# Linear attention and MLP on one core: squares of the decay taken early, two transposed tiles copied by two engines, three store pairs merged

## The chip, the cores and the metric

The kernel runs on one core of a Trainium2 chip. The metric is the device time of that core in microseconds (us); lower is better. A *time* below is that of a whole execution; a *span* is the stretch from the first to the last instruction in a trace, and the time is about 1.8 us longer (200.52 us beside a span of 198.7 us for the kernel before).

## The reference, cut to what matters

Linear attention with one decay factor per head, in blocks of 64 tokens, followed by a two-layer MLP.

```python
# q, k, v: (4 batches, 8 heads, 768 tokens, 64); lam: (8,), 0.97 to 0.99
for b in range(12):                      # blocks of 64 tokens
    intra = (qb @ kb.T * Dmask) @ vb      # Dmask = lam**(i - j), 0 above the diagonal
    inter = (qb * lam_pow) @ kv_state
    out[block] = intra + inter
    kv_state = lam**64 * kv_state + (kb * rev_pow).T @ vb
# x: (3072, 512), the heads of a token side by side
h = x @ w_in                              # (3072, 2048)
g = 0.5*h*(1 + tanh(c*(h + 0.044715*h**3)))
return g @ w_out                          # (3072, 512) float32
```

## The kernel before

The attention runs in 24 steps of 128 tokens. The start of the kernel computes powers of lam: `dq` for q, its inverse `dv` for v, and lam to the 128th (seven squarings) as the decay of the state, which is laid out as a masked tile `lumask` and a plain tile `lamu`. Each step multiplies q by `dq` (VectorE), copies k (ScalarE), multiplies v by `dv` (GpSimd). For steps 0 to 8, TensorE then transposes q and k into the PSUM tile `Tps`, and a copy moves them to `qkT` in SBUF. The MLP's matmuls fill TensorE from about 16 us on.

```python
    def square(i):
        pin(nc.vector.tensor_tensor(sq[i + 1][:], sq[i][:], sq[i][:], ALU.mult))

    def odd(hs):
        pin(nc.vector.tensor_tensor(dq[:, hs, 1], dq[:, hs, 0], lam_bc[:, hs], ALU.mult))

    def chunk_decay():                                   # the state's decay, 4 elements a partition
        l3 = sq[7][:].rearrange("p (hp two) -> p hp two", two=2)
        for hl in range(2):
            r = slice(64 * hl, 64 * hl + 64)
            pin(nc.vector.tensor_copy(out=lumask[r, :, hl], in_=l3[r, :, hl]))
        pin(nc.vector.tensor_tensor(lamu[:], lumask[:, :, 0], lumask[:, :, 1], ALU.add))

    for i in range(5):
        square(i)
    odd(halves[0])
    # ... cut ...
    def stage_t(s):                                      # transposes of step s and their copy
        # ... cut: eight transposes into Tps, which is one PSUM tile: q into Tps[:, 0], k into Tps[:, 1]
        o = qkp.tile([P, 2, 2, 2, P], FP16, tag="qkT", name=f"qkT_{s}")
        if s in (2, 3):
            pin(nc.scalar.activation(out=o[:, 0], in_=Tps[:, 0], func=AF.Copy))
            pin(nc.vector.tensor_copy(out=o[:, 1], in_=Tps[:, 1]))
        elif s in (1, 5, 6, 8):
            pin(nc.scalar.activation(out=o[:], in_=Tps[:], func=AF.Copy))
        else:
            pin(nc.vector.tensor_copy(out=o[:], in_=Tps[:]))
    # ... cut ...
            def store(T, ps=slice(0, NP), es=slice(0, 2)):   # output tile T of token group g
                r = row0 + T * HN
                rows = out[r : r + HN, :].rearrange("(p q) (e d) -> q p e d", q=P, e=2)
                for i in range(ps.start, ps.stop):           # one transfer of 256 KB each (128 KB for half of es)
                    pin(nc.sync.dma_start(out=rows[:, i, es], in_=out_tile(T)[:, i, es, :]))
    # ... cut: the order of the work from here ...
    idle(4)              # matmuls on ones, whose result nobody reads: they keep TensorE busy
    prep(0)              # q, k, v of step 0
    stage_t(0)
    idle(1)
    square(5)
    square(6)
    prep(1)
    chunk_decay()
    idle(2)
    R(0, None)           # scores, products and mask of step 0
    stage_t(1)
    idle(5)
    # ... cut ...
```

`pin` keeps the order of the program on each engine.

## Time and profile before

| | kernel before |
|---|---|
| time, median of six (beside the kernel after) | 201.07 us (200.94 to 201.34) |
| profiled execution: time, span | 200.52 us, 198.7 us |
| TensorE busy | 191.4 us of 198.7 (96%) |
| stores of the output | 23 transfers of 256 KB and two of 128 KB; the last store is one of the two |

The list of DMA issues (output and input, queue, count, size, median us from issue to landing) has the stores that the change merges:

```profile
out_dram<-o SPq DMA_DIRECT2D x23, 256.0 KB, 4.2
```

First, the idle matmuls of the first 13 us (the view of one source line: count, then durations in ns as shortest / median / longest, then the first and the last start in us). One of 512 columns takes about 635 ns before TensorE's clock rises and 380 after (back to back, one starts every 0.43 us before the rise and every 0.22 us after it), so the median tells that most of them ran after the rise:

```profile
L182 PE MATMUL idle<-ones x19: 379/380/635, 1.5 to 11.7; 128*128 128x512 f16 x19
```

Second, three pieces of the chain that ended last (start us, us, engine, tile, line): the first long run of MLP matmuls (24.50 here; the timeline, which the prediction reads, has its first matmul at 24.34), then the transposes of step 4, where the prediction expected a delay to be absorbed, and what follows them:

```profile
24.50 6.91 PE Hps L524 x32
...
39.17 0.61 PE Tps L293 x8
...
39.78 1.73 PE O2ps L539 x8
```

### The profile page before, as it was taken

The page shows a single profiled execution, that of the slowest core. Times are in us where ns is not written, and L with a number is a line of the kernel's source. Part 1 is how long each engine was busy: PE and PEld are TensorE (multiplying, and loading weights), DVE is VectorE, ACT ScalarE, POOL GpSimd, SP SyncE. Part 2 cuts the span into 40 slices and gives each one's busy share as a digit, 9 for nine tenths or more (in the row PEclk, how much of TensorE's full clock was granted, in tenths as well). Part 3 has the DMA queues.
Part 4 walks back from the last instruction along what each step waited for, and adds up shares of the span by engine and source line. Part 5 has one row for each costly group of instructions (what it writes and reads, how often), then busy time and mean ns, then how long its engine had stood idle before and what let it go on. Part 6 is the DMA issues. An engine that isn't in the chain of part 4 may idle for free.

```text
span 198.7 us, 5952 instructions
## 1 busy us (share of the span) xinstructions
PE 191.4 (96%) x2444; PEld 139.2 (70%) x2444; DVE 153.3 (77%) x299; ACT 122.1 (61%) x246; POOL 73.6 (37%) x85
## 2 busy tenths in 40 slices
PE   7889999999999999999999999999999999999992
PEld 1446544456888898654588754578888888888881
DVE  5898723689999889949898478999768996588530
ACT  2463878466883674587735577844768845779211
POOL 6593223457457733435633465055002030002000
PEclk9999999999999999999999999999999999999999
DMA  6999999999999999999774999340220300020214
GB/s 172 290 326 386 385 386 384 295 286 310 333 254 253 235 297 216 237 290 215 190 174 93 278 294 200 86 51 0 53 85 24 108 6 0 0 109 16 93 46 167
DMA packets 61755, 37.87 MB, mean 191 GB/s; under 512 B 17568, under 2 KB 54688, under 8 KB 61728
## 3 DMA queue, kind: packets, MB, share of 16 engines
q1 hardware_dynamic: 61184, 37.23, 72.4%
q8 instruction: 19, 0.31, 0.7%
q10 hardware_dynamic: 544, 0.26, 0.5%
q14 instruction: 8, 0.07, 0.1%
HBM read 27.26 MB, written 6.29 MB: 169 GB/s over the span
## 4 chain that ended last, share of the span: by engine, by line
PE 93%; DVE 2%; ACT 1%; POOL 1%; issue 1%
PE Hps L524 24%; PE MX L601 17%; PE MY L601 9%; PE HX L692 7%; PE O2ps L539 7%; PE MW L601 4%; PE Hps L783 4%; PE S L322 4%; PE HY L692 4%; PE OK L380 2%; PE Tps L293 2%; PE OK L371 2%; PE HW L692 2%; PE idle L182 1%; POOL dq L216 1%; PE OK L357 1%
## 5 line engine op out<-in xcount | busy, mean ns | idle before, releaser
L524 PE MATMUL Hps<-xT,w_in 128*128 128x512 f16 (+1 forms) x288 | 51.0, 332 | 0.0
L483 POOL TENSOR_TENSOR u<-t,lumask 128x256 f16<-128x256 f32 x40 | 29.9, 761 | 49.1 <-DVE t L476 33.7
L524 PEld LDWEIGHTS <-w_in 128*128 128x128 f16 x288 | 27.8, 98 | 18.8
L528 ACT ACTIVATE gT<-Hps 128x512 f16<-128x512 f32 x56 | 33.0, 596 | 10.9 <-PE Hps L524 10.4
L332 DVE TENSOR_TENSOR PT<-S,mask 128x512 f16<-128x512 f32 x48 | 30.5, 682 | 8.0 <-PE S L322 7.9
L601 PEld LDWEIGHTS <-gs 128*128 128x128 f16 x320 | 31.2, 98 | 3.6
L257 POOL TENSOR_TENSOR v<-v,dv 128x512 f16<-128x512 f32 x24 | 29.6, 1239 | 6.9 <-DMA v<-in_v_dram 6.5
L601 PEld LDWEIGHTS <-gT 128*128 128x128 f16 x240 | 23.2, 98 | 3.6 <-ACT gT L528 0.5
L601 PE MATMUL MX<-w_sum,gs 128*128 128x256 f16 x160 | 21.4, 273 | 0.0
L275 ACT ACTIVATE qk<-k 128x512 f16<-128x512 f32 x24 | 15.0, 626 | 7.6 <-DMA k<-in_k_dram 7.6
L270 DVE TENSOR_TENSOR qk<-q,dq 128x512 f16<-128x512 f32 x23 | 19.1, 832 | 0.5 <-DMA q<-in_q_dram 0.5
L645 POOL TENSOR_TENSOR o<-u,q 128x512 f32<-128x512 f32 (+1 forms) x5 | 5.3, 1054 | 37.8 <-ACT u L618 37.8
L571 DVE TENSOR_TENSOR gs<-gT 128x1024 f16<-128x1024 f16 (+1 forms) x24 | 17.8, 749 | 1.7 <-ACT gT L528 1.7
L457 ACT ACTIVATE xT<-OK 128x256 f16<-128x256 f32 x34 | 13.0, 456 | 6.4 <-PE OK L380 6.2
L539 PE MATMUL O2ps<-w_out,gT 128*128 128x512 f16 x64 | 14.6, 379 | 0.0
L692 PEld LDWEIGHTS <-ws 128*128 128x128 f16 x128 | 12.5, 97 | 1.8
L618 ACT ACTIVATE u<-MX 128x256 f32<-128x256 f32 x18 | 6.9, 383 | 10.1 <-PE MX L601 10.1
L476 DVE SCALAR_TENSOR_TENSOR t<-t,lamu,OK 128x64 f32<-128x64 f32 x48 | 11.0, 275 | 1.1 <-PE OK L357 0.2
L322 PEld LDWEIGHTS <-qkT 64*64 64x64 f16 x384 | 6.1, 106 | 7.5 <-issue 2.3
L539 PEld LDWEIGHTS <-gT 128*128 128x128 f16 x64 | 6.1, 98 | 6.6
L601 PE MATMUL MY<-w_out,gs 128*128 128x256 f16 x80 | 10.7, 273 | 0.0
L601 PE MATMUL MX<-w_sum,gT 128*128 128x256 f16 x80 | 10.4, 273 | 0.0
(94 smaller groups left out, 311.8 us busy)
## 6 DMA issues: line engine op xcount, KB each, us to landing
q<-in_q_dram SPq DMA_DIRECT2D x24, 256.0 KB, 5.2
k<-in_k_dram SPq DMA_DIRECT2D x24, 256.0 KB, 5.1
v<-in_v_dram SPq DMA_DIRECT2D x23, 256.0 KB, 5.3
out_dram<-o SPq DMA_DIRECT2D x23, 256.0 KB, 4.2
wo<-in_moe_w_out_dram SPq DMA_DIRECT2D x4, 1024.0 KB, 9.5
wi<-in_moe_w_in_dram SPq DMA_DIRECT2D x4, 512.0 KB, 8.0
wi<-in_moe_w_in_dram SPq DMA_DIRECT2D x2, 1024.0 KB, 12.7
v<-in_v_dram ACTq DMA_DIRECT2D x1, 256.0 KB, 4.2
```

The source lines that it names most:

```text
L257: pin(nc.gpsimd.tensor_tensor(wide(tv[:]), ld32[s][2][:], decay(dv, s), ALU.mult))
L270: pin(q_eng.tensor_tensor(wide(tq), q32[:], decay(dq, s), ALU.mult))
L275: pin(nc.scalar.activation(out=wide(tk), in_=k32[:], func=AF.Copy))
L322: pin(nc.tensor.matmul(Sps[hl][half64(c), hp, jk, :], o[half64(hl), 1, jk, hp, half64(c)], o[half64(hl), 0, :, hp, half64(c)], start=True, ...
L332: pin(nc.vector.tensor_tensor(t[:, hl].rearrange("p b c d -> p b (c d)"), Sps[:].rearrange("p b c d -> p b (c d)"), mask[:].unsqueeze(1).t ...
L483: pin(nc.gpsimd.tensor_tensor(u[:], state[half][:].unsqueeze(2).to_broadcast([P, 2, 2, D]), lumask[:, 2 * half : 2 * half + 2, :].unsqueez ...
L524: pin(nc.tensor.matmul(by_block(Hps[:, i, :]), w_in16[:, c, f * P : (f + 1) * P], x(c), start=(c == 0), stop=(c == NC - 1)))
L528: pin(nc.scalar.activation(out=dst, in_=Hps[:], func=AF.Gelu_apprx_tanh))
L539: pin(nc.tensor.matmul(O2[tau][0][:], gT[:, f % HF, f // HF, tau * P : (tau + 1) * P], w_out16[:, f, :], start=(n == 0), stop=(n == NF - 1)))
L571: pin(nc.vector.tensor_tensor(g_rows(m, i), g_rows(a, i), g_rows(b, i), op))
L601: pin(nc.tensor.matmul(dst, lhsT, rhs, start=(opens and i == 0), stop=(closes and i == HF - 1), skip_group_check=True))
L692: pin(nc.tensor.matmul(dst[:, i, :], w_in_block(a, slice(c, c + 1), slice(f * P, f * P + P))[:, 0], x_block(b, slice(c, c + 1))[:, 0], sta ...
```

## The change

Three intents. The last two squarings move ahead of step 0, and ScalarE instead of VectorE spreads the result into `lumask` and `lamu`, so that VectorE is freed between q of step 0 and q of step 1. The copies of `Tps` in steps 0 and 1 are split into a ScalarE and a VectorE half, as steps 2 and 3 already were. And three pairs of output transfers become one transfer of 512 KB each.

```diff
     def chunk_decay():
         l3 = sq[7][:].rearrange("p (hp two) -> p hp two", two=2)
-        for hl in range(2):
-            r = slice(64 * hl, 64 * hl + 64)
-            pin(nc.vector.tensor_copy(out=lumask[r, :, hl], in_=l3[r, :, hl]))
-        pin(nc.vector.tensor_tensor(lamu[:], lumask[:, :, 0], lumask[:, :, 1], ALU.add))
-
-    for i in range(5):
+        for dst in (lumask, lamu):
+            for hl in range(2):
+                r = slice(64 * hl, 64 * hl + 64)
+                to = lamu[r, :] if dst is lamu else lumask[r, :, hl]
+                pin(nc.scalar.activation(out=to, in_=l3[r, :, hl], func=AF.Copy))
+
+    for i in range(7):
         square(i)
     odd(halves[0])
@@
-        if s in (2, 3):
+        if s < 4:
             pin(nc.scalar.activation(out=o[:, 0], in_=Tps[:, 0], func=AF.Copy))
             pin(nc.vector.tensor_copy(out=o[:, 1], in_=Tps[:, 1]))
-        elif s in (1, 5, 6, 8):
+        elif s in (5, 6, 8):
@@
-                for i in range(ps.start, ps.stop):
+                whole = g == 3 or (g, T) == (4, 0)
+                for i in [ps] if whole else [slice(i, i + 1) for i in range(ps.start, ps.stop)]:
                     pin(nc.sync.dma_start(out=rows[:, i, es], in_=out_tile(T)[:, i, es, :]))
@@
     stage_t(0)
+    chunk_decay()
     idle(1)
-    square(5)
-    square(6)
     prep(1)
-    chunk_decay()
     idle(2)
```

## The prediction

> **What bounds the kernel now.** I read the page first, then the chain that ended last, then the start and the stretch around 39 us of the timeline. The page says who is busy and when:
>
> ```profile
> PE 191.4 (96%) x2444; PEld 139.2 (70%) x2444; DVE 153.3 (77%) x299; ACT 122.1 (61%) x246; POOL 73.6 (37%) x85
> ...
> PE   7889999999999999999999999999999999999992
> ...
> DMA  6999999999999999999774999340220300020214
> ...
> PE 93%; DVE 2%; ACT 1%; POOL 1%; issue 1%
> ```
>
> TensorE (PE) is full from the fourth slice on: a slice is 198.7 / 40 = 4.97 us, so only about the first 15 us have holes, and the last slice is the final store. The chain (last line) agrees. The DMA engines are at nine tenths or more from slice 2 to slice 19, which will matter. The change can therefore only pay in the first 20 us, where a step runs VectorE (q times decay) and ScalarE (k copied), eight TensorE transposes into Tps, the copy of Tps to qkT, then the scores S. The timeline of that stretch (start and duration in us, engine, line; in brackets the idle time before it and its releaser):
>
> ```profile
> 4.47 0.16 DVE L224 TENSOR_TENSOR dq<-dq,lam_bc 128x4 f32<-128x4 f32 x1
> 4.67 0.69 DVE L270 TENSOR_TENSOR qk<-q,dq 128x512 f16<-128x512 f32 x1
> ...
> 5.42 0.69 PE L293 MATMUL Tps<-ident,qk 128*128 128x128 f16 x8 [0.48 <-POOL dq L216]
> ...
> 6.14 0.69 DVE L302 COPY qkT<-Tps 128x1024 f16<-128x1024 f16 x1 [0.29 <-PE Tps L293]
> ...
> 6.75 0.36 DVE L221 TENSOR_TENSOR sq<-sq 128x8 f32<-128x8 f32 x2
> 6.88 0.26 PEld L322 LDWEIGHTS <-qkT 64*64 64x64 f16 x16 [0.63 <-DVE qkT L302]
> ...
> 7.44 0.63 ACT L275 ACTIVATE qk<-k 128x512 f16<-128x512 f32 x1 [1.79 <-DMA k<-in_k_dram]
> ...
> 8.55 1.02 ACT L300 ACTIVATE qkT<-Tps 128x1024 f16<-128x1024 f16 x1 [0.49 <-PE Tps L293]
> ...
> 9.63 0.26 PEld L322 LDWEIGHTS <-qkT 64*64 64x64 f16 x16 [0.53 <-ACT qkT L300]
> ...
> 11.51 0.60 ACT L297 ACTIVATE qkT<-Tps 128x512 f16<-128x512 f16 x1
> ...
> 12.14 0.42 DVE L298 COPY qkT<-Tps 128x512 f16<-128x512 f16 x1
> ```
>
> The two evictions to be split are at 6.14 (step 0, VectorE alone, 0.69 us) and 8.55 (step 1, ScalarE alone, 1.02 us); the scores of both wait for them. The last two lines are step 2, already split in the way the change uses: the ScalarE half ends at 12.11 and the VectorE half starts at 12.14. The halves run one after the other. VectorE's work before that copy (masking PT, from 10.72 for 1.27 us) had ended at 11.99, so the 0.15 us between is a wait for ScalarE. The built program of the changed kernel says the same: VectorE's half waits for ScalarE's semaphore in all four split steps.
>
> Then the place where the start meets the rest of the kernel:
>
> ```profile
> 38.70 0.63 ACT L275 ACTIVATE qk<-k 128x512 f16<-128x512 f32 x1 [0.75 <-DMA k<-in_k_dram]
> 38.80 0.42 PEld L293 LDWEIGHTS <-qk 128*128 128x128 f16 x4
> 39.01 0.77 PE L293 MATMUL Tps<-ident,qk 128*128 128x128 f16 x8
> 39.38 0.23 PEld L293 LDWEIGHTS <-qk 128*128 128x128 f16 x4 [0.16 <-ACT qk L275]
> ```
>
> At 38.70 ScalarE has just been given k of step 4 by a DMA; four of that step's transposes are ready, the other four wait 0.16 us for ScalarE's copy. So TensorE already arrives there 0.16 us early, and the DMA queue, saturated since about 5 us, says when it may go on.
>
> [...]this trace has 0.21 us for the one-element warm-up activation, and I use that, rounded to 0.2, for the four tiny spreads. [...] The holes here are 0.3 to 0.5 us and the page's granted clock is 9 tenths or more throughout, [...].
>
> **The change part by part.**
>
> Squares early. Before, five squares run from 3.35 to 4.33, then the odd decay waits for GpSimd's power (3.40 + 1.01 = 4.41) and starts at 4.47. Squares are 0.20 us apart (3.35, 3.56), so seven end at 4.73 and the odd decay starts at 4.76: 0.29 later. q of step 0 then ends at 5.65 instead of 5.36. Its transposes took 0.69, partly waiting for k (ScalarE, done 5.65); that wait goes and they take 0.62, as in step 2: they end at 6.32, not 6.11. Cost 0.21.
>
> First eviction. 0.69 becomes 0.60 + 0.03 + 0.42 = 1.05, cost 0.36. The scores of step 0 start at about 7.45, not 6.88: 0.57 later.
>
> VectorE afterwards. The two late squares (0.36) are gone, so q of step 1 starts at 7.40, not 7.03. ScalarE does the four spreads from 6.97 to 7.8 and reaches k of step 1 at 7.8, while its DMA landed at 7.44: a new delay of 0.36. The transposes of step 1 end at about 8.8 against 8.51, 0.3 later. Against this VectorE has lost three small instructions (two of 0.16 us and one of 0.16 us, from 7.63 to 8.15), so the masking of step 0 and the state copy keep their old times, 8.05 and 9.25.
>
> Second eviction. ScalarE's half 8.82 to 9.42, VectorE's half, behind the state copy, 9.45 to 9.87: the scores of step 1 at about 9.92 instead of 9.63. So 1.02 us on one engine becomes 1.05 on two, and the sum so far is a loss of 0.3.
>
> Down the rest of the start. Steps 2 and 3 are copied as before and inherit 0.3, except where a DMA rules: k of step 3 (12.82), v of step 3 (16.53) and the second half of the first weights (17.82) are all waited for now. In the last, eight matmuls took 1.05 us although eight of 256 columns take 0.87 elsewhere (the 49.34 piece of the chain), so about 0.1 is swallowed there. From 20 us TensorE has no hole and carries 0.2 us to 39 us. There the 0.16 us wait for k swallows nearly all. The next step's transposes (0.55 in the chain against 0.45 for later ones) may take up another few hundredths. Left at the end: 0 to 0.1 us.
>
> Stores. Three pairs of 256 KB transfers become one of 512 KB each, same bytes and same 2 KB rows. Saved: three issues of 0.37 us (median) on SyncE's queue, which nothing in the late kernel waits for; the next transposes by DMA are issued at 116.93 for scores wanted after 126. The final group keeps its stores. I count 0.
>
> Sum: 201.01 + about 0.05, so 201.05 us.
>
> **The rivals.** (a) The whole loss of 0.3 to 0.57 reaches the end, because the k wait at 39 us is released earlier than I think or ScalarE itself runs late there. For: a full TensorE passes any delay on. Against: k lands at 38.70 whatever the start does, as the casts that free the weight buffers are themselves waiting for DMA (25.93 for the last). It would give 201.3 to 201.6. (b) The change works as intended: halves overlap or the lighter VectorE shortens the chain, the start gains 0.2 to 0.3. For: VectorE loses 0.5 us of small work before the mask of step 0 and ScalarE idles 1.79 us before k. Against: the serial halves; and even then k at 38.70 holds the gain back. It would give 200.8 to 201.0. (c) Fewer, larger stores disturb or relieve the loads near 105 to 120 us. DMA is at 2 to 4 tenths there, so at most 0.1 either way. (d) The longer hole drops the clock [...], unlikely at such short holes.
>
> **Range and chances.** The three runs of before span 0.19 us. My central 201.05 with (b) as the lower edge plus noise and (a) as the upper gives 200.7 to 201.6. Two per cent is 4 us, more than the whole start has in holes, so within 2% has 0.98, and each side 0.01.
>
> **What would show it.** Right: the step-0 scores begin near 7.4, VectorE's half starts 0.03 us after ScalarE's half in steps 0 and 1, ScalarE takes k of step 1 near 7.8 with no DMA wait, the long run of matmuls from 24.3 is 0.1 to 0.3 late, and at 39.4 the k transposes wait less than 0.16 us or not at all, with everything after where it was. Wrong: the two halves overlap; the small ScalarE copies take 0.1 or 0.4; TensorE is late after 45 us by as much as at 24 us; or a new wait stands near 105 to 125 us.

## More of the kernel before

The framework closes the kernel when its tile context is left: SyncE then waits on the semaphores of the DMA transfers (in the trace of this kernel five waits on two semaphores each, begun from 195.85 to 197.45 us). That code is not the kernel's own, and the argument will come to it.

The end: the last ScalarE copy of an output tile in the timeline,

```profile
195.05 0.38 ACT L618 ACTIVATE o<-MX 128x256 f32<-128x256 f32 x1 [0.49 <-PE MX L601]
```

and SyncE's closing instructions, on the line that leaves the tile context, in the view of one source line:

```profile
L1041 SPq EVENT_SEMAPHORE  x7: 17/28/1345, 195.8 to 198.7; - x7
L1041 SPq DRAIN  x3: 7/7/122, 197.8 to 198.3; - x3
```

One of SyncE's seven semaphore waits took 1345 ns, and the first drain begins at 197.8, 122 ns long. The last copy ends at 195.43 and the span at 198.75, which is 3.31 us for the last store and the closing.

## The result, and the profile after

| | before | after |
|---|---|---|
| median of six executions, us | 201.07 | 200.43 |
| lowest to highest, us | 200.94 to 201.34 | 200.02 to 200.69 |
| ratio, 95% interval | | 0.9964 [0.9949, 0.9979] |
| profiled execution: time, span | 200.52, 198.7 | 200.68, 198.9 |

A ratio here and below is the mean time of one kernel's fast runs over that of the other's in the same rounds, so it is not quite the ratio of the medians. The kernel after is 0.64 us faster by the medians: within 2%, but just under the predicted range of 200.7 to 201.6, and on the other side of the time before.

The two profiled executions say the opposite, 0.16 us slower. That is no contradiction: before's is faster than each of its six timed executions (200.94 at the least), after's the second slowest of its six. Two traces must be read for where they differ, and the parts then weighed with the timed executions. The trace differs in three places.

The page first; it answers the prediction's first block:

```profile
PE 192.6 (97%) x2444; PEld 140.4 (71%) x2444; DVE 150.4 (76%) x297; ACT 122.8 (62%) x251; POOL 73.4 (37%) x85
...
PE   7889999999999999999999999999999999999993
...
PE 93%; DVE 3%; ACT 1%; issue 1%
```

TensorE has 1.2 us more of busy time for the same 2444 matmuls. As no matmul was added, some ran slower. Nothing else on the page gives a reason; its row of the granted clock shows nine tenths or more throughout, in both kernels.

**The start.** The timeline of the kernel after (columns as in the prediction):

```profile
4.65 0.16 DVE L224 TENSOR_TENSOR dq<-dq,lam_bc 128x4 f32<-128x4 f32 x1
...
5.58 1.04 PE L294 MATMUL Tps<-ident,qk 128*128 128x128 f16 x8 [0.65 <-DVE qk L271]
...
6.66 0.60 ACT L298 ACTIVATE qkT<-Tps 128x512 f16<-128x512 f16 x1 [0.90 <-PE Tps L294]
...
7.15 0.41 ACT L235 ACTIVATE lumask<-sq 64x4 f32<-64x4 f32 x2
...
7.29 0.42 DVE L299 COPY qkT<-Tps 128x512 f16<-128x512 f16 x1 [1.38 <-ACT qkT L298]
...
7.83 0.64 PE L323 MATMUL S<-qkT 64*64 64x128 f16 x16
...
8.03 0.63 ACT L276 ACTIVATE qk<-k 128x512 f16<-128x512 f32 x1
...
10.78 0.42 PE L323 MATMUL S<-qkT 64*64 64x128 f16 x16
```

VectorE's half of step 0 starts at 7.29, 0.03 us after ScalarE's half ends (7.26), and the same holds in step 1: the halves are serial. Two spreads take 0.41 us, and k of step 1 starts at 8.03 with no DMA wait. All this the prediction had. But the eight transposes at 5.58 took 1.04 us where before's took 0.69, and the sixteen score matmuls 0.64 where before's took 0.42. No wait stands between them; TensorE was at half clock: the idle matmuls among them, from 6.41 to 7.27, start every 0.43 us, and those from 9.68 every 0.22. The idle matmuls (the same view as before) say so too, by their median of 606 ns against 380:

```profile
L182 PE MATMUL idle<-ones x19: 379/606/634, 1.5 to 12.7; 128*128 128x512 f16 x19
```

The raw clock records of the trace give the moment of the rise: 4.87 us in the profiled execution of before, 9.48 us in that of after. The start lost 1.00 us in all (chain, the run of 32 matmuls at 25.50 and not 24.50), of which the late rise is one part and the work moved by the change another.

**At 39 us.** The chain, and from the timeline ScalarE's copy of k of step 4:

```profile
25.50 6.91 PE Hps L525 x32
...
40.18 0.45 PE Tps L294 x8
...
40.62 1.73 PE O2ps L540 x8
```

```profile
38.90 0.63 ACT L276 ACTIVATE qk<-k 128x512 f16<-128x512 f32 x1 [0.75 <-DMA k<-in_k_dram]
```

The transposes of step 4 now take 0.45 us and not 0.61: k is ready well before TensorE comes, its 0.16 us wait is gone, and the loss shrinks from 1.00 to 0.84. That is the absorption that the prediction described, by the amount it gave. The rest, 0.84 us, stays.

**The end.** It stays until the last copy of an output tile, which is 0.87 us late:

```profile
195.92 0.38 ACT L619 ACTIVATE o<-MX 128x256 f32<-128x256 f32 x1 [0.49 <-PE MX L602]
```

And yet the span is only 0.15 us longer, 198.90 against 198.75. From the end of that copy to the end of the span, before took 3.31 us and after takes 2.60: **0.71 us came back behind the last instruction that computes anything.** SyncE's closing instructions:

```profile
L1041 SPq EVENT_SEMAPHORE  x7: 17/28/28, 196.7 to 198.8; - x7
L1041 SPq DRAIN  x3: 7/7/13, 198.1 to 198.4; - x3
```

There is no long wait and no long drain. The last store itself was no faster: from the end of its issue to its completion as SyncE sees it, 1.40 us before and 1.43 after. The list of DMA issues shows the merged stores,

```profile
out_dram<-o SPq DMA_DIRECT2D x17, 256.0 KB, 3.5
out_dram<-o SPq DMA_DIRECT2D x3, 512.0 KB, 4.8
```

but these leave the core long before: the last of them is issued at 147.98 us. What they changed is how many transfers there are: 123 before, 120 after. The records of the DMA-issuing instructions carry the semaphore that each transfer raises, and these come from a ring of eight, in the fixed order 100, 102, 103, 105, 106, 107, 108, 109. With 123 transfers the last store gets the third of the ring, 103; with 120 it gets the eighth, 109. SyncE's closing code waits for them in pairs, in the same order in both traces. From the raw records, in us:

```
closing wait on       before: wait over at   after: wait over at
105 and 103           197.19  (last store)   196.7 to 196.9
106 and 102           197.2 to 197.5,        196.7 to 196.9
107 and 100             four more waits,     196.7 to 196.9
108 and 101             0.07 apart           197.5
109 and 110                                  198.08  (last store)
pause                 0.37                   0.04
first drain ends      197.97                 198.13
last store seen -> drain ends   0.78         0.05
drain ends -> span ends         0.78         0.77
```

So before, the store that finishes last is the first to be waited for, and the four waits, the pause and the drain of the closing all come after it. After, four of the five pairs of waits are done while the last store is still under way, and pause and drain add 0.05 us. The theory for the experiments, called the ring theory below: *the gain is the place of the last store in the ring; the start loses a little, and the late clock is chance.* Its rivals: the transfer theory, that larger and fewer transfers themselves relieve something; the start theory, that the start pays in most executions and the profiled one of after is unlucky; and the hole theory, that the longer hole before the first transposes (0.65 us against 0.49) delays the rise of the clock, so that the change causes it.

### The profile page after: what moved, and what is told of

It is laid out like the page before. It is cut to its first block, busy times and chain, and to the rows that moved or that the text cites.

```text
span 198.9 us, 5947 instructions
## 1 busy us (share of the span) xinstructions
PE 192.6 (97%) x2444; PEld 140.4 (71%) x2444; DVE 150.4 (76%) x297; ACT 122.8 (62%) x251; POOL 73.4 (37%) x85
## 4 chain that ended last, share of the span: by engine, by line
PE 93%; DVE 3%; ACT 1%; issue 1%
PE Hps L525 24%; PE MX L602 17%; PE MY L602 9%; PE HX L694 7%; PE O2ps L540 7%; PE MW L602 4%; PE S L323 4%; PE Hps L785 4%; PE HY L694 4%; PE Tps L294 2%; PE OK L381 2%; PE OK L372 2%; PE HW L694 2%; PE idle L182 1%; PE OK L358 1%; PE O L432 1%
## 5 line engine op out<-in xcount | busy, mean ns | idle before, releaser
L258 POOL TENSOR_TENSOR v<-v,dv 128x512 f16<-128x512 f32 x24 | 30.1, 1258 | 5.6 <-DMA v<-in_v_dram 3.7
L271 DVE TENSOR_TENSOR qk<-q,dq 128x512 f16<-128x512 f32 x23 | 18.6, 813 | 0.6 <-DMA q<-in_q_dram 0.6
```

Of the source, the lines that this page charges most:

```text
L258: pin(nc.gpsimd.tensor_tensor(wide(tv[:]), ld32[s][2][:], decay(dv, s), ALU.mult))
L271: pin(q_eng.tensor_tensor(wide(tq), q32[:], decay(dq, s), ALU.mult))
```

## The experiments

Each kernel was timed in rounds beside the kernel before on the same chip; kernels of one group share those runs of before. All outputs are right. By the rule of a 2% threshold every run below counts as the same as the kernel before; the intervals say what can be told apart. The expectations are quoted as they were before each run and may call a theory by another name. The first group is a1_stores to a4_tiny1 (before: 200.71), the second a5_split5 to b4_fill (before: 200.72), the third the rest (before: 201.08).

### The stores alone

```diff
 # the kernel before, with only the third hunk of the change
+                whole = g == 3 or (g, T) == (4, 0)
+                for i in [ps] if whole else [slice(i, i + 1) for i in range(ps.start, ps.stop)]:
-                for i in range(ps.start, ps.stop):
```

> The kernel before with the three merged store pairs alone; the start is untouched. Theory (the end of the kernel): 120 DMA transfers in place of 123 shift the ring of eight DMA semaphores by three, the last store gets the semaphore that SyncE's closing waits check last (109) in place of one that they check first (103), and the time from the last ScalarE copy to the end falls from 3.31 to about 2.6 us: 200.3 to 200.5 us, ratio 0.996 to 0.998. Rival (the start): all of the gain is made in the first 20 us and this run is at 201.0, ratio 1.000.

Measured: 200.17 us (200.08 to 201.26) beside 200.71, ratio 0.998 [0.9959, 1.0001]. One execution of six, 201.26, is a microsecond above the other five, which lie at 200.08 to 200.48, and widens the interval past 1; the times alone leave it unclear. The trace does not: the start is before's (long run at 24.52), and the closing is after's. The last copy ends at 195.73, the span at 198.32, 2.58 us, with the drain at 197.6 and no long wait:

```profile
L1042 SPq EVENT_SEMAPHORE  x7: 17/28/28, 196.1 to 198.3; - x7
```

### The start alone

The kernel after with the old store loop, the same hunk reversed.

> The changed kernel with the stores as before; only the two parts in the start. Theory: 123 transfers again, so the closing time is 3.3 us as before, and the start costs 0.2 us where TensorE's clock rises at about 5 us and 0.85 us where it rises only at about 9.5 us: 201.2 to 201.9, ratio 1.001 to 1.005. Rival: the start gains, 200.4, ratio 0.997.

Measured: 201.01 us (200.51 to 201.41), ratio 1.0013 [0.9994, 1.0031]. The closing is long again, 3.31 us, with its long wait:

```profile
L1040 SPq EVENT_SEMAPHORE  x7: 17/28/1360, 196.7 to 199.6; - x7
```

The start of the profiled execution is after's, at 25.53, with the clock rising at 9.53 us. So the start brings nothing at the end of the kernel and probably costs some tenths. The start theory falls.

### Same stores, other counts

If only the count matters, transfers that carry nothing should do as well. Five loads of 32 bytes, into a tile that nobody reads, make 128 transfers, so the last store is again the eighth of the ring; one load makes 124, the fourth. The transfer theory expects no gain of either, since no store is merged.

```diff
+    spare = const.tile([H, 8], FP32)
@@ late in the kernel, long before the last stores
+    for i in range(5):        # a3_tiny5;   range(1) in a4_tiny1
+        pin(nc.sync.dma_start(out=spare[:, i : i + 1], in_=lam.unsqueeze(1)))
     fill(20)
```

> The kernel before, start and stores untouched, with five loads of 32 bytes that nobody reads added near 140 us: 128 transfers, which by eight is the same place in the semaphore ring as 120. Theory (ring): the last store has semaphore 109 and the closing time falls to about 2.6 us although there are more transfers, not fewer: 200.3 to 200.5, ratio 0.996 to 0.998. Rival (fewer, larger stores help by themselves): no gain, 201.0, ratio 1.000 or a little over.

> As the run with five tiny loads, but one: 124 transfers, the last store has semaphore 105, which the first of the closing waits checks, as with 103 before. Theory (ring): closing time 3.3 us, 201.0, ratio 0.999 to 1.001. Rival (any shift of the instruction stream helps): 200.4.

Measured, beside 200.71: a3_tiny5 201.09 us (200.01 to 201.86), ratio 1.0018 [0.9995, 1.0041]; a4_tiny1 201.58 us (200.63 to 201.91), ratio 1.0029 [1.0005, 1.0052]. In the traces the closing follows the ring exactly: 2.61 us with five loads, 3.26 us with one. SyncE's closing with one load, where the last store raises 105 and so is in the first pair:

```profile
L1044 SPq EVENT_SEMAPHORE  x7: 17/28/28, 197.3 to 198.7; - x7
L1044 SPq DRAIN  x3: 7/7/35, 198.0 to 198.3; - x3
```

Its seven waits begin only at 197.3, and the drain follows 0.7 us later, as in before; with five loads they begin at 196.3. The profiled executions agree with that, 200.01 against 200.63 us. But four of the five other executions of each lie 0.86 us or more above the profiled one, and by the medians neither is faster than before: the times that the theory expected (200.3 to 200.5 with five loads, 201.0 with one) were missed. (The recorded ratio of a3_tiny5 seems to leave out its fastest run; the means of the listed times give 1.0008.) Between the two kernels the medians differ by 0.49 us in the expected direction, but their intervals overlap. What the small loads cost in those other executions I could not see, since only one execution of each kernel has a trace; it stays open. For that reason a cleaner way to 128 transfers followed.

```diff
 # a5_split5: five stores cut in two instead of three pairs merged
-                    pin(nc.sync.dma_start(out=rows[:, i, es], in_=out_tile(T)[:, i, es, :]))
+                    for e in (slice(0, 1), slice(1, 2)) if g == 3 or (g, T, i) == (4, 0, 0) else (es,):
+                        pin(nc.sync.dma_start(out=rows[:, i, e], in_=out_tile(T)[:, i, e, :]))
```

> The kernel before with five of its late stores cut in two each (rows of 1 KB in place of 2 KB), nothing else: 128 transfers, by eight the same place in the ring as 120. Theory (ring): from the end of the last ScalarE copy to the end of the span 2.6 us in place of 3.31, and the time as with the merged stores, 0.5 to 0.7 us under the kernel before of the same rounds (ratio 0.9965 to 0.9985). Rival (larger stores help, more and smaller ones harm): ratio 1.000 or above, closing time 3.3 us. The two runs with tiny loads showed the shorter and the longer closing time in the profile, but their timed executions were mostly 1 us longer than the profiled one, so this run repeats the test without tiny loads.

Measured: 200.24 us (200.15 to 201.82) beside 200.72, ratio 0.9985 [0.9957, 1.0013]. More and smaller stores, the opposite of the change, and the median moves by the same half microsecond as with merged ones, though the interval includes 1. The closing took 2.89 us: the last store itself took 1.73 us from the end of its issue, 0.3 longer than elsewhere, and behind it there was again no long wait. So a shorter closing needs neither fewer nor larger transfers, and for the closing the ring theory stands. That larger transfers relieve nothing elsewhere is not shown by these times. The profiled execution of this kernel, which has before's start untouched, had the clock rise at 9.38 us: that speaks against the hole theory, at least as the only cause.

The closings of all fourteen traces, from raw records (last copy's end to the span's end):

```
kernel      transfers   last store raises   closing us
before      123         103 (third)         3.31
a2_start    123         103                 3.31
b1_split    123         103                 3.31
b2_decay    123         103                 3.30
a4_tiny1    124         105 (fourth)        3.26
after       120         109 (eighth)        2.60
r_after     120         109                 2.60
a1_stores   120         109                 2.58
b4_fill     120         109                 2.58
b3_banks    120         109                 2.58
c2_idle5    120         109                 2.59
c1_best     120         109                 2.58
a3_tiny5    128         109                 2.61
a5_split5   128         109                 2.89
```

Only the third, fourth and eighth place of the ring were tried.

### The halves alone

```diff
 # the kernel before, with only the second hunk of the change
-        if s in (2, 3):
+        if s < 4:
@@
-        elif s in (1, 5, 6, 8):
+        elif s in (5, 6, 8):
```

> The kernel before with the halves of steps 0 and 1 alone; squares, spreads and stores as before. Theory (serial halves): VectorE's half of step 0 starts about 0.03 us after ScalarE's half ends and the scores of step 0 begin 0.36 us later than before; the hole of TensorE before step 0's transposes stays 0.49 us, so the clock still rises by 7.9 us at the latest; TensorE is 0.1 to 0.4 us late at the first group of 512-wide matmuls (24.34 before). Closing time 3.3. Ratio 1.000 to 1.002. Rival (halves overlap): scores of step 0 earlier than 6.88 and ratio under 0.999.

Measured: 202.29 us (201.15 to 202.43), ratio 1.0058 [1.0034, 1.0083]: slower by about 1.2 us on the mean, more than any other kernel here. The timeline shows what happened:

```profile
8.44 1.19 DVE L233 COPY lumask<-sq 64x4 f32<-64x4 f32 x2
...
8.56 1.04 POOL L257 TENSOR_TENSOR v<-v,dv 128x512 f16<-128x512 f32 x1 [1.66 <-DVE qk L270]
```

The two spreads of four elements took 1.19 us on VectorE; by the view of that line one took 155 ns, the other 1019 ns, and it ended as GpSimd's multiplication of v did. In the kernel before both ran ahead of that multiplication:

```profile
7.63 0.33 DVE L233 COPY lumask<-sq 64x4 f32<-64x4 f32 x2
```

That VectorE was held up there by GpSimd is my reading of this one trace: the same copy took 155 ns just before the multiplication and 1019 ns beside it, and ended with it. Why it waited was not shown. The scores of step 1 started at 11.61 and not 9.63. The clock has a part too: it rose at 9.13 us in this trace, where the expectation had said 7.9 at the latest. The long run of matmuls started at 26.23, 1.73 us later than before; beside a5_split5, which has before's start and a rise at 9.38, it is 0.87 later. a2_start, which has these halves with the spreads on ScalarE and the early squares, starts its long run at 25.53 with the clock as late, and does not show the loss (ratio 1.0013). So by these traces moving the spreads to ScalarE is what makes the split halves bearable: on VectorE they came late enough to run into GpSimd's v (8.44 to 9.63 us, beside 8.56 to 9.60), while on ScalarE in the kernel after they run from 7.15 to 8.01, ahead of that v at 8.48. The prediction had priced the spreads alone and never asked what they would meet.

### The decay alone

a2_start with the two lines of the halves put back.

> The kernel before with the early squares and ScalarE's spreads alone; evictions and stores as before. Theory: the hole of TensorE before step 0's transposes grows from 0.49 to 0.65 us, so in those executions [...] the clock rises at 9.5 us; elsewhere it rises by 7.9 us. Ratio 1.000 to 1.004, with executions in two groups some 0.6 us apart. Rival (the lighter VectorE shortens the start): ratio 0.998.

Measured: 200.80 us (200.55 to 201.73) beside 200.72, ratio 1.0008 [0.9982, 1.0034]. The scores of step 1 started at 9.74, 0.11 later than before; the long run of matmuls at 24.79, with the clock rising at 6.78.

### The hole filled

The hole theory says that the hole before the first transposes delays the clock. One more idle matmul fills it.

```diff
 # the kernel after
-    idle(4)
+    idle(5)
     prep(0)
```

> The changed kernel with one more idle matmul (five in place of four) in the hole before step 0's transposes: nothing computed differs. Theory (clock): [...] the clock rises by 7.9 us at the latest in every execution, the executions lie in one group, and TensorE is only 0.2 to 0.4 us late at 24 us; with the closing time of 2.6 us this gives 0.3 to 0.5 us under the kernel before of the same rounds, ratio 0.9975 to 0.9985, and less spread than the changed kernel. Rival (the clock has no part; the start is late through ScalarE and VectorE alone): TensorE 0.8 to 1.0 us late at 24 us, ratio 0.999 to 1.001.

Measured: 200.15 us (199.97 to 200.24) beside 200.72, ratio 0.9963 [0.9945, 0.9981]. The clock rose at 6.55 us in its trace, and the long run began at 25.07, 0.43 ahead of the profiled execution of after. The range of its six times, 0.27 us, is the narrowest of all. The gain is larger than expected (0.9975 to 0.9985).

### The kernel after again, and with two PSUM tiles

r_after is the kernel after, unchanged, for a second sample on the chip of the third group. b3_banks gives the two halves of the transposes of steps 0 to 3 a PSUM tile each (two banks, in the words of the expectations), to let ScalarE and VectorE copy at the same time.

```diff
 # b3_banks: the kernel after
-        Tps = ps_M.tile([P, 2, 2, 2, P], FP16, tag="M", name="Tps")
+        halves_T = [ps_M.tile([P, 2, 2, P], FP16, tag="M", name=f"T{i}") for i in range(2)]   # s < 4
 ... transposes into halves_T[i][:, j, hp, :] ...
-            pin(nc.scalar.activation(out=o[:, 0], in_=Tps[:, 0], func=AF.Copy))
-            pin(nc.vector.tensor_copy(out=o[:, 1], in_=Tps[:, 1]))
+            pin(nc.scalar.activation(out=o[:, 0], in_=halves_T[0][:], func=AF.Copy))
+            pin(nc.vector.tensor_copy(out=o[:, 1], in_=halves_T[1][:]))
```

> The changed kernel once more, on the chip of the other runs, as the base for the next three. Theory: closing time 2.6 us in every execution; the start late by 0.3 us where the clock rises by 7.9 us and by about 0.9 us where it rises near 9.5 us; so executions between 0.6 us under the kernel before and level with it, ratio 0.9965 to 0.9995.

> The changed kernel with the transposes of q and of k of steps 0 to 3 in two PSUM tiles, that is in two banks; the copies are the same. The built program then has VectorE's half wait for TensorE in place of ScalarE. Theory (one bank makes the halves serial): VectorE's half of step 0 starts within 0.1 us of its transposes and not after ScalarE's half, the scores of step 0 start 0.4 to 0.6 us earlier than in the changed kernel at the same clock, and TensorE is 0.2 us or more earlier at 24 us; little of that reaches the end, since k of step 4 lands at 38.8: 0.0 to 0.3 us under the changed kernel. Rival (something else holds VectorE's half, the destination tile for one): no change in the order of the halves.

Measured: r_after 200.53 us (200.26 to 201.65) beside 201.08, ratio 0.9977 [0.9949, 1.0004]; b3_banks 200.33 us (199.89 to 200.96), ratio 0.9965 [0.9942, 0.9988]. The kernel after repeats its gain of half a microsecond by the medians. With two tiles the halves do overlap:

```profile
6.23 0.60 ACT L302 ACTIVATE qkT<-T 128x512 f16<-128x512 f16 x1 [0.38 <-PE T L298]
...
6.66 0.42 DVE L303 COPY qkT<-T 128x512 f16<-128x512 f16 x1 [0.75 <-PE T L298]
```

ScalarE runs to 6.83, and VectorE starts at 6.66 on a release by TensorE and not by ScalarE. With one tile it starts 0.03 us after ScalarE's half ends. So it was the shared tile that made them serial; tile and bank were not told apart. The expected earlier scores of step 0 did not come: they start at 7.83 in this trace and in that of after, both with a late clock, behind the three idle matmuls that TensorE has before them. At the end nothing of it can be told from r_after, whose interval overlaps. The prediction's reason, that k of step 4 rules at 39 us, fits this; but the clock, which rose at 9.04 in this trace, differs too, so it is no clean proof.

The trace of r_after has a loss of another kind. In its chain k of step 10 lands only at 57.94:

```profile
51.42 6.52 DMA k<-in_k_dram
58.02 0.63 ACT qk L276
```

This execution took 200.86 us, 0.3 more than its kernel's median, although its clock rose at 7.38. The DMA engines are still at nine tenths there; whether late transfers also cost time in other executions was not seen.

### The best of both

The stores of the change and the filled hole, on before's start; and the same with the halves in two tiles in steps 0 to 3.

```diff
 # c2_idle5: a1_stores with          # c1_best: c2_idle5 with the two tiles of b3_banks
-    idle(4)
+    idle(5)
     prep(0)
```

> The kernel before with the merged stores and one more idle matmul before step 0's transposes. Theory: closing time 2.6 us, the clock up by 7.9 us at the latest, TensorE at 24.3 to 24.8 us at the first group of wide matmuls: 0.6 to 0.8 us under the kernel before, ratio 0.996 to 0.997, executions in one group. Rival (late clock depends on something else): executions 0.6 us or more apart, and a clock that rises after 9 us in the profile or in part of the executions.

> As the last run, with the halves of steps 0 to 3 in two banks as well (squares and spreads as before). Theory: the start gains another 0.2 to 0.4 us at 24 us, but four transposes of step 4 then wait longer for k at 39 us (0.3 us or more in place of 0.16), so the end gains nothing: within 0.15 us of the last run. Rival (the start sets the end): 0.2 to 0.4 us faster than the last run. Third way: VectorE's small copies meet GpSimd's v and the start loses, as in the run with the halves alone.

Measured: c2_idle5 200.12 us (200.02 to 200.39), ratio 0.9951 [0.9933, 0.9969]; c1_best 200.21 us (199.85 to 200.28), ratio 0.995 [0.9931, 0.9969]. Both beat the kernel before clearly, and by the medians the kernel after in the same group (200.53) by 0.3 to 0.4 us. Between them there is no difference, although in the traces c1_best started its long run at 25.09 and c2_idle5 at 24.73: the expected gain of the two tiles at 24 us did not come (VectorE's half of step 1 started only at 9.57, and the scores of step 1 at 10.04 against 9.59 in c2_idle5), and the 0.36 us do not show in the medians, 0.09 apart. So half of the change's text, the start, is not needed: c2_idle5 has none of it, only the stores and one idle matmul more.

### The clock, over all traces

```
kernel      hole before first transposes   clock rises at us   long run at us
a1_stores   as before (0.49 us)             4.51               24.52
before      as before                       4.87               24.50
a4_tiny1    as before                       6.44               24.76
a3_tiny5    as before                       7.43               24.79
b1_split    as before                       9.13               26.23
a5_split5   as before                       9.38               25.36
b2_decay    changed                         6.78               24.79
r_after     changed                         7.38               24.96
b3_banks    changed                         9.04               25.00
after       changed (0.65 us)               9.48               25.50
a2_start    changed                         9.53               25.53
c2_idle5    filled                          5.62               24.73
b4_fill     filled                          6.55               25.07
```

Kernels with the old start have late rises too (9.13, 9.38), so the change is not needed for them. Two of six traces with the old start have one and three of five with the changed start: too few to say whether the changed start makes them likelier, which stays open of the hole theory. (c1_best has no such record in its trace.) Near the end of each trace, with TensorE idle again, the clock falls (at 199.43 us in that of before, at 200.62 in that of after), 191.146 or 194.56 us after its rise. The two differ by 3.413 us and are 56 and 57 times that. From these two durations alone I estimate that the clock changes only at moments that lie 3.413 us apart, and the scatter of the rises, 4.51 to 9.53 us with the first matmul at 1.45, then tells that each execution meets these periods at another phase. The late rises, 9.0 and more, less one such period give 5.6 to 6.1 us: if the estimate holds, the clock could have risen there and did not, with the hole inside the period that ended there; in c2_idle5, which has no hole there, it did rise at 5.62. What makes it rise was not shown. By its matmul records TensorE was busy for 0.81 to 0.86 of a period that so ended without a rise (0.81 in the trace of after, from 2.65 to 6.06 us), but later periods with the same shares ended with one (0.81 in b2_decay, from 3.37 to 6.78). What did differ is the period before: it was busy for 0.22 to 0.37 of its time ahead of the former, and for 0.46 to 0.75 ahead of those that ended with a rise at such shares. Whether that decides was not tested. The 7.9 us of the expectations was an estimate of mine; the rises that were not late lie at 4.51 to 7.43 us.

A late rise costs 0.86 us at 24 us (a5_split5 at 25.36 against before at 24.50, the same start). Where the clock rises at about the same time, the changed start costs 0.2 to 0.3 us (24.96 to 25.07 against 24.76 to 24.79) when the rise is at 6.4 to 7.4, and 0.14 (25.50 against 25.36) when it is at 9.4.

That fits part of the scatter, though the clock of only one execution of each kernel is on record: the six times of an unfilled kernel spread over as much as 1.8 us (a3_tiny5, 200.01 to 201.86), while the three with five idle matmuls, 18 executions, all lie between 199.85 and 200.39. At most a part: the late transfer of r_after may be another source, and I saw no trace of the slowest executions.

## Why the prediction was right or wrong

**Wrong: the stores.** The step that failed is "Saved: three issues of 0.37 us (median) on SyncE's queue, which nothing in the late kernel waits for … I count 0." It counted bytes, issues and waits of the kernel, and left out the closing, where SyncE waits on the transfers' semaphores in the same order in both traces. The term measured -0.71 us (3.31 to 2.60), and it is the sign and nearly the whole size of the result. The same step named the wrong suspect in rival (c), disturbed loads at 105 to 120 us. The signs were in the trace of before: the wait of 1345 ns, the four waits, the pause and the long drain after it, and the count of transfers. The prediction read the last slice of the page as "the final store" and stopped there.

**Right: the serial halves.** VectorE's half starts 0.03 us after ScalarE's in both steps, and with two tiles it does not wait for it (6.66, ScalarE's half ending at 6.83).

**Right: the spreads,** 0.41 us for two on ScalarE, and k of step 1 at 8.03 (predicted near 7.8) with no DMA wait.

**Right in sign, and in size where the clock rises alike: the start.** "From 20 us TensorE … carries 0.2 us to 39 us" was 0.14 to 0.3 us in the pairs of traces above. The scores of step 0 were predicted near 7.45 and stood at 7.83, since the matmuls before them ran at half clock (634 ns for one idle matmul, not 380). Those of step 1 were predicted 0.29 later (9.92, not 9.63) and stood at 10.78; with the rise at 7.4 in both, r_after has 10.25 and a3_tiny5, with before's start, 9.87. Of the working, the odd decay starts at 4.65 and not at 4.76, so the early squares cost 0.11 less than counted. The "about 0.1" said to be swallowed at 18 us sets 1.05 us from the timeline beside 0.87 from the chain; the chain has 0.98 for the same eight matmuls, and the 0.1 stands. The mask and the state copy before were at 8.07 and 9.27, not 8.05 and 9.25, which changes nothing.

**Right: the absorption at 39 us,** 0.16 us, the wait that the prediction had read there. With 0.1 to 0.3 lost and 0.16 given back, "0 to 0.1 us left" fits; but the traces cannot show so small a rest, and a2_start (1.0013, with 1 inside its interval) cannot either.

**Underrated: the clock.** Rival (d) was called "unlikely at such short holes". In the trace of before a hole of 0.49 us came right after the rise and the clock stayed up (379 to 380 ns for each idle matmul behind it); how long a hole it stands was not shown. A late rise stood in five of thirteen traces with a recorded rise, and cost 0.86 us in the one clean pair. It was not the change that dropped it, as the rival had it: the clock had not yet risen. The prediction took the granted-clock row of the page as proof that the start ran at full clock, though before's own idle matmuls of up to 635 ns showed that at least some of it had not. The clock is late in traces of both starts. Its moment in the timed executions is not on record, so a part of the 0.64 us may be a different share of late rises in the two samples; the difference of the closings does not depend on it.

**"Everything after where it was"** held for the gain at 39 us and not for the profiled execution, which carried 0.84 us on to the end, all from the late clock and the start.

The sum, with measured terms: closing -0.71, start about +0.2, absorbed about -0.16, so some -0.67 us; measured -0.64 by the medians. The last two are near the scatter, the median of before itself was 200.71, 200.72 and 201.08 us in the three groups, and the clock adds its own, so such a close agreement is partly luck.

## What to carry to other kernels

Read the last microseconds behind the last computing instruction as a stage of its own: which semaphore the last transfer raises, and where in the closing order it is waited for. Here a change in the mere number of DMA transfers moved it by 0.7 us, so a gain or loss of that size must not be credited to the transfers themselves until the count has been varied without them. And when two profiled executions disagree with the medians, look for matmuls of the same shape with different durations (here 606 ns against 380, by the median) before looking for waits.

## What stays open

- The end of a kernel: the runs show 3.26 to 3.31 us of closing with the last store on the third or fourth of the ring of eight and 2.58 to 2.61 us (2.89 once) on the eighth. Why a pause of 0.37 us stands between the last wait and the drain in the kernel before is not settled; in a4_tiny1 it stands before the fourth pair of waits.
- The clock: with the first matmul at 1.45 us the runs show its rise at 4.51 to 9.53 us. What decides the moment is not settled. Executions with a hole of 0.49 or 0.65 us had it at 9.0 to 9.5 us, and others with the same holes by 7.43; with one more idle matmul (634 ns) the times of three kernels stayed within 0.6 us.
